# Gated linear attention and a channel MLP on one core: the first product in 15 products for 18, and scores that follow the update of the batch ahead

## The chip, the cores and the metric

The kernel runs on one core of a Trainium2 chip. The metric is the device time of one execution in microseconds (us). The engines are TensorE (PE in the profile, with its weight loads as PEld), VectorE (DVE), ScalarE (ACT), GpSimd (POOL) and SyncE (SP), which issues the DMAs.

## What is computed

The reference has two parts. The first is recurrent attention with a decay per element, for 4 batches, 8 heads, 768 positions and head size 48:

```
for t in range(S):
    state = alpha[:, :, t, :, None] * state + np.einsum('bhd,bhe->bhde', k[:, :, t], v[:, :, t])
    y[:, :, t] = np.einsum('bhd,bhde->bhe', q[:, :, t], state)
```

y becomes x of shape (4, 768, 384), and the second part is

```
xn = (x - mu) / np.sqrt(var + 1e-06) * g_ln
ch = np.maximum(xn @ w_ch1, 0.0) @ w_ch2
return x + ch
```

with mean and variance over the 384 features, w_ch1 of 384 x 1536 and w_ch2 of 1536 x 384. The weights arrive as 64-bit floats and are rounded to fp32 on the chip; everything else is fp32.

## The kernel before

**Tiles.** The 768 positions are cut into 6 chunks of 128. `attention(c, b)` (L205) is a generator that does one chunk of one batch in 16 pieces: logarithm of alpha (la); its running sum as a matmul with a triangle (lps) and two exponentials; k times one of them on GpSimd (L218); q times the other on VectorE (L220) and one row to DRAM; the loads of the next chunk's alpha, k, q, v (L227); two transposes (tps, L233, to qkT); the scores (aps, L245); their masked copy (L249); the row back as gate columns (L254); y (yps, L262 and L267); the state's update as a matmul (sps, L277); the update's sum on VectorE (L282) and its product with the gate on GpSimd (L284); statistics; the normalised x (xn, L295); its transpose into xT (L302).

**First product** (x times w1, then Relu, into hT). For chunks 0 and 1 `hidden` (L308) does 12 blocks of 3 matmuls of 512 columns. For chunks 2 to 5 `hidden_product` (L453) uses Winograd's form of Strassen's scheme on two of the three feature blocks: batches in halves, hidden blocks in halves, 7 products of a pair of blocks, of which 4 take the third feature block along in a second matmul. One group is 7 products, 22 matmuls of 256 columns; a chunk has 3 groups. `combine_first` (L404) makes the weights' sums on GpSimd; `combine_x` (L436) makes those of xT on VectorE at each chunk's start. Products leave PSUM by VectorE sums (L473, L481, L482, L484, L488) or ScalarE copies (L471, L475, L478), some are added further on GpSimd (L476, L479), and ScalarE does the Relu in place (L486, L490).

**Second product** (hT times w2). For chunk 0 `project` (L322) is direct; for chunks 1 to 5 `product` (L361) does Strassen's 7 products for each pair of batches, 6 matmuls of 192 columns each (L371). `combine_weights` (L337) makes w2's sums on GpSimd, `combine_hidden` (L349) those of hT on VectorE.

**Order.** The start (attention of chunks 0 and 1, rounding of the weights, `hidden(0)`) follows a string written by hand, ORDER, of one letter per piece (L23, L536). From then on `run(main, side)` (L523) goes through the main steps (second product of chunk c, first product of chunk c+1) and puts side steps (pieces of the attention of chunk c+2) between them in proportion. `attention_steps` (L495) gives 20 side steps: stages of 5, 2, 3, 5 and 1 pieces, with batch b one stage behind batch b-1. These calls set priorities; the tile framework then lays out each engine's order, in which an instruction that is ready can go ahead of one written earlier. An example: the logarithm of chunk 2's first batch runs at 34.59 us, while the first product of chunk 0 begins at 40.76.

**Buffers.** A tile's tag has a number of buffers; a new tile waits until an old one's last reader is done. a, k and q have 4 buffers each, v has 8 (L101). `combine_first` takes 2 of each of them for good, for its new sums. The 'm' tag of PSUM has 3 buffers, used by both products. hT has one.

Of the kernel before, what the change touches and what calls it, by code (L numbers as in the profile page):

```python
# [30 lines left out]
def kernel(  # L31
# [34 lines left out]

    nc = tc.nc
# [29 lines left out]
    def load(c, b, names="akqv"):  # L97
        for n, src in (("a", alpha), ("k", k), ("q", q), ("v", v)):
            if n not in names:
                continue  # L100
            t = raw.tile([P, H, D], FP32, name=f"r{n}", tag=f"r{n}",  # L101
                         bufs=2 * B if n == "v" else B)
            nc.sync.dma_start(t, src[b, c * P:(c + 1) * P])
            raws[n, c, b] = t
# [100 lines left out]
    def attention(c, b):  # L205
# [20 lines left out]
        if c + 1 < NCB:  # L226
            load(c + 1, b)  # L227
# [52 lines left out]
        if c + 1 < NCB:  # L280
            for i, s in heads:
                nc.vector.tensor_add(sts[b][s, :, i], sps[s], sts[b][s, :, i])  # L282
            st = sts[b].rearrange("p a b d -> p a (b d)")
# [53 lines left out]
    def combine_weights():  # L337
        b11, b12 = w2[:, :HJ, :HM], w2[:, :HJ, HM:]
        b21, b22 = w2[:, HJ:, :HM], w2[:, HJ:, HM:]
        t1, t2, t4 = (stage.tile([P, NF, 2 * P], INT64, name="ws", tag="ws")  # L340
                      .rearrange("p a c -> p (a c)").bitcast(FP32)[:, :HJ * HM]
                      .rearrange("p (a c) -> p a c", c=HM) for _ in range(3))
# [6 lines left out]
    def combine_hidden(c, b):  # L349
# [3 lines left out]
        sums = work.tile([P, 3, HJ, P], FP32, name="sums", tag="sums", bufs=1)  # L353
        s2, s3, s4 = (sums[:, i] for i in range(3))
# [6 lines left out]
    def product(c, b, n):  # L361

        if n == 1:
            combine_hidden(c, b)
            for i in (0, 1):
                win["o", i] = work.tile([P, 2, HM], FP32, name="ob", tag="ob", bufs=3)
            for i in range(4):
                win["u", i] = work.tile([P, HM], FP32, name=f"u{i}", tag=f"u{i}", bufs=1)
# [33 lines left out]
    HB = B // 2  # L402

    def combine_first():  # L404
        a11, a12 = w1[:, 0, :HJ * P], w1[:, 1, :HJ * P]
        a21, a22 = w1[:, 0, HJ * P:], w1[:, 1, HJ * P:]
        d1, d2 = w1[:, 2, :HJ * P], w1[:, 2, HJ * P:]
        parts = [[raw.tile([P, H, D], FP32, name=f"r{n}", tag=f"r{n}",
                           bufs=2 * B if n == "v" else B).rearrange("p h d -> p (h d)")
                  for _ in range(2)] for n in "akqv"]  # L410
        half = HJ // 2 * P

        def sub(outs, x, y):
            for i, o in enumerate(outs):
                cs = slice(i * half, (i + 1) * half)
                nc.gpsimd.tensor_sub(o, x[cs] if isinstance(x, list) else x[:, cs], y[:, cs])

        def blocks(x):
            if isinstance(x, list):
                return lambda j: x[j // (HJ // 2)][:, j % (HJ // 2) * P:][:, :P]  # L420
            return lambda j: x[:, j * P:(j + 1) * P]

        s2, s3, s4, dd = parts
        sub(dd, d1, d2)
        sub(s3, a11, a21)
        nc.gpsimd.tensor_add(a21, a21, a22)
        sub(s2, a21, a11)
        for i, o in enumerate(s4):
            nc.gpsimd.tensor_sub(o, a12[:, i * half:(i + 1) * half], s2[i])
        first_of["a"] = {n: blocks(x) for n, x in  # L430
                         ((1, a11), (2, a12), (3, s4), (4, a22), (5, a21), (6, s2), (7, s3))}
        first_of["d"] = {n: blocks(x) for n, x in ((2, d1), (3, dd), (4, d2), (5, d2))}

    first_of = {}

    def combine_x(c):  # L436
        xT = xT_of[c].rearrange("p f b t -> p f (b t)")
        lo, hi = slice(0, HB * P), slice(HB * P, B * P)
        b11, b12, b21, b22 = xT[:, 0, lo], xT[:, 0, hi], xT[:, 1, lo], xT[:, 1, hi]
        t = work.tile([P, 3, HJ * P], FP32, name="xs", tag="sums", bufs=1)  # L440
        t = t.rearrange("p a b -> p (a b)")
        t1, t2, t4 = (t[:, i * HB * P:(i + 1) * HB * P] for i in range(3))
        for i in range(3):
# [130 lines left out]
```

## Time and profile before

| | us |
|---|---|
| median of 3 runs | 496.3 |
| lowest and highest | 496.2, 497.53 |
| the profiled execution's own time | 495.51 |
| its span (first to last instruction) | 493.7 |

The mean granted TensorE clock of that execution was 0.999. A line of the profile gives the line of the code, the engine, the operation, tile written <- tiles read, shape and count; then busy time and mean duration of one, and behind a bar the engine's idle time just before such instructions, with what ended most of it. The chain of waits, followed back from the last instruction, is 79% TensorE, 13% VectorE, 4% DMA and 2% ScalarE; its largest parts are L371 (28%), L463 (15.4%), L466 (8.4%) and L313 (7.6%). TensorE's first instruction waits for alpha at 5.25 us.

### The profile page before, as it was taken

What the parts mean: (1) busy time and instruction counts of PE and PEld (TensorE: products, weight loads), DVE (VectorE), ACT (ScalarE), POOL (GpSimd) and SP (SyncE); (2) the same over time, 40 slices, a digit from 0 to 9 for tenths busy, and PEclk for the clock granted to TensorE, in tenths of its full rate; (3) what the DMA queues carried; (4) which work ended last, traced back from release to release, by engine and by line L of the source; (5) the groups of instructions that cost most, each with busy time, mean ns of one, the idle gap of its engine ahead of it and who ended that gap; (6) DMA issues with size and microseconds to landing.
All of it is one profiled execution on the core that took longest, in us unless ns stands there. A gap on an engine that the chain in (4) does not pass through costs nothing.

```text
span 493.7 us, 9035 instructions
## 1 busy us (share of the span) xinstructions
PE 477.2 (97%) x3712; PEld 385.9 (78%) x3712; DVE 284.0 (58%) x478; ACT 152.8 (31%) x325; POOL 131.7 (27%) x132
## 2 busy tenths in 40 slices
PE   4989999979999999999999999999999999999997
PEld 2766465546555599988889988889998889998997
DVE  4799998882433357565475555555654445443551
ACT  5573452530212221143441134342124431024300
POOL 5052000155210128532222222223123222222321
PEclk9999999999999999999999999999999999999999
DMA  8995726312200002211003212001200000000000
GB/s 281 342 243 174 256 91 201 109 50 65 65 2 1 29 5 64 81 56 28 17 18 118 52 56 65 1 1 32 66 33 2 1 0 1 34 32 1 1 33 32
DMA packets 32497, 33.83 MB, mean 69 GB/s; under 512 B 13108, under 2 KB 28596, under 8 KB 32456
## 3 DMA queue, kind: packets, MB, share of 16 engines
q1 hardware_dynamic: 31912, 33.12, 21.5%
q8 instruction: 29, 0.48, 0.4%
q10 hardware_dynamic: 544, 0.13, 0.1%
q14 instruction: 12, 0.10, 0.1%
HBM read 28.49 MB, written 4.76 MB: 67 GB/s over the span
## 4 chain that ended last, share of the span: by engine, by line
PE 79%; DVE 13%; DMA 4%; ACT 2%; issue 1%; SPq 0%; DVEq 0%; ACTq 0%
PE ops L371 28%; PE hps L463 15%; PE hps L466 8%; PE hps L313 8%; PE ops L326 4%; PE aps L245 4%; PE yps L267 3%; PE yps L262 3%; PE tps L233 3%; DVE ws L156 2%; DMA ws<-in_moe_w_ch_dram 2%; PE lps L212 2%; DVE w L163 2%; DVE w L150 1%; DVE at L249 1%; DVE w L159 1%
## 5 line engine op out<-in xcount | busy, mean ns | idle before, releaser
L313 PE MATMUL hps<-xT,w 128*128 128x512 f32 x144 | 66.1, 600 | 0.3 <-DVE w L163 0.2
L284 POOL TENSOR_TENSOR st<-st,gate 128x384 f32<-128x384 f32 x20 | 18.0, 899 | 127.2 <-DVE st L282 60.9
L313 PEld LDWEIGHTS hps<-xT,w 128*128 128x128 f32 x144 | 25.9, 190 | 27.8 <-issue 24.2
L371 PE MATMUL ops<-w,hT 128*128 128x192 f32 x240 | 44.1, 329 | 0.0
L466 PE MATMUL hps<-xT,w 128*128 128x256 f32 x144 | 42.8, 379 | 0.0
L371 PE MATMUL ops<-ws,hT 128*128 128x192 f32 x240 | 42.6, 326 | 0.0
L371 PE MATMUL ops<-w,sums 128*128 128x192 f32 x240 | 42.6, 327 | 0.0
L371 PEld LDWEIGHTS ops<-w,hT 128*128 128x128 f32 x240 | 39.2, 190 | 2.1 <-ACT hT L490 0.6
L371 PEld LDWEIGHTS ops<-w,sums 128*128 128x128 f32 x240 | 39.4, 190 | 1.8
L371 PEld LDWEIGHTS ops<-ws,hT 128*128 128x128 f32 x240 | 39.6, 190 | 0.0
L218 POOL TENSOR_TENSOR qk<-rk,ek 128x384 f32<-128x384 f32 x24 | 26.7, 1111 | 41.6 <-ACT ek L215 41.6
L249 DVE COPY_PREDICATED at<-consts,aps 128x512 f32<-128x512 int32 x48 | 32.3, 723 | 7.6 <-PE aps L245 7.4
L326 PE MATMUL ops<-w,hT 128*128 128x384 f32 x96 | 33.7, 494 | 2.7 <-DVE w L159 2.3
L476 POOL TENSOR_TENSOR xs<-xs 128x512 f32<-128x512 f32 x12 | 15.2, 1267 | 78.3 <-ACT xs L475 78.3
L267 PE MATMUL yps<-rv,at 128*64 128x48 f32 x768 | 35.8, 219 | 0.3 <-ACT x L270 0.3
L220 DVE TENSOR_TENSOR qk<-rq,eq 128x384 f32<-128x384 f32 x24 | 22.5, 942 | 23.0 <-ACT eq L216 23.0
L267 PEld LDWEIGHTS yps<-rv,at 128*64 128x64 f32 x768 | 31.6, 138 | 1.1 <-DMA ra<-in_alpha_dram 0.5
L282 DVE TENSOR_TENSOR st<-sps,st 64x192 f32<-64x192 f32 (+1 forms) x40 | 14.2, 354 | 29.6 <-PE sps L277 29.1
L466 PEld LDWEIGHTS hps<-xT,w 128*128 128x128 f32 x144 | 27.4, 190 | 3.7
L245 PEld LDWEIGHTS aps<-qkT 48*128 48x128 f32 x384 | 23.8, 187 | 8.3 <-issue 5.5
L326 PEld LDWEIGHTS ops<-w,hT 128*128 128x128 f32 x96 | 17.4, 190 | 14.7 <-DVE w L159 3.5
L262 PE MATMUL yps<-st,qkT 112*64 112x96 f32 x320 | 28.8, 258 | 0.0
(98 smaller groups left out, 849.3 us busy)
## 6 DMA issues: line engine op xcount, KB each, us to landing
ws<-in_moe_w_ch_dram SPq DMA_DIRECT2D x12, 768.0 KB, 8.4
ra<-in_alpha_dram SPq DMA_DIRECT2D x24, 192.0 KB, 3.1
rk<-in_k_dram SPq DMA_DIRECT2D x24, 192.0 KB, 2.4
rq<-in_q_dram SPq DMA_DIRECT2D x24, 192.0 KB, 2.5
rv<-in_v_dram SPq DMA_DIRECT2D x24, 192.0 KB, 2.9
out_dram<-ob SPq DMA_DIRECT2D x24, 192.0 KB, 2.3
row<-eq SPq DMA_DIRECT2D x20, 2.0 KB
gate<-row SPq DMA_DIRECT2D x20, 2.0 KB, 3.1
```

What stands on the lines that cost most here:

```text
L218: nc.gpsimd.tensor_mul(qk[:, 1, :, :D], raws.pop(("k", c, b)), ek)
L220: nc.vector.tensor_mul(qk[:, 0, :, :D], raws.pop(("q", c, b)), eq)
L245: nc.tensor.matmul(aps[i][:, p], qkT[rows, 1, p], qkT[rows, 0, p], start=True, stop=True)
L249: nc.vector.copy_predicated(out=at[:, i], data=aps[i], mask=mask.unsqueeze(1).broadcast_to([P, NP, P]))
L262: nc.tensor.matmul(yps[s, p].rearrange("p a b -> p (a b)"), qkT[:, 0, p, s], sts[b][:R, p].rearrange("p a b -> p (a b)"), start=True, stop ...
L267: nc.tensor.matmul(yps[s, p, i], at[:, i, p, s], vt[:, 2 * p + i], start=(c == 0), stop=(c == 0 or i == 1))
L284: nc.gpsimd.tensor_mul(st, st, gate.unsqueeze(2).broadcast_to([P, NP, 2 * D]))
L313: nc.tensor.matmul(hps, w1[:, f, j * P:(j + 1) * P], xT_of[c][:, f], start=(f == 0), stop=(f == NF - 1))
L326: nc.tensor.matmul(ops_of[b], hT_of[c][:, j, b], w2[:, j], start=(j == 0), stop=(j == NJ - 1))
L371: nc.tensor.matmul(acc, win["a"][n][:, j], win["b"][n][:, j], start=(j == 0), stop=(j == HJ - 1))
L463: nc.tensor.matmul(acc[:, i], first_of["a"][n](j + i), first_of["b"][n], start=True, stop=n not in first_of["d"])
L466: nc.tensor.matmul(acc[:, i], first_of["d"][n](j + i), first_of["x"][n], start=False, stop=True)
```

## The change

It has these parts:

1. **First product in 15 products for 18.** Features are cut in thirds (the three feature blocks), hidden blocks in thirds (4 each), batches in halves. A direct product of such blocks is 3 x 3 x 2 = 18 block products; the new scheme has 15. `hidden_product(c, r, n)` does one product of two hidden blocks as 2 matmuls of 256 columns; a chunk has 2 groups (r) of 15. It is used from chunk 1 on (before: from chunk 2). A group before had 7 + 4 matmuls per block, which is 11 of 12.
2. **Sums.** `combine_first` has 17 sums or differences of w1's blocks on GpSimd, each as two instructions of 384 and 128 columns; 6 new blocks lie in two buffers each of a, k and q (and a small tile for the remaining columns), the rest in place of w1. It is called ahead of chunk 0's run, not after it. `combine_x` has 11 VectorE instructions of 256 columns for 4.
3. **Evictions.** Of 15 products 12 leave by a VectorE instruction and 3 by a ScalarE copy; 7 further sums are on GpSimd; 6 Relus of two instructions of 256 columns follow. The order of the products is FIRST.
4. **Tiles.** `combine_hidden`'s three sums get a tile each for one together, two of which `combine_x` takes again; the small u tiles are laid into three of 512 columns; the weights' staging tiles are taken once, as `spare`.
5. **combine_weights** becomes a step between chunk 0's second product and chunk 1's first.
6. **v** is loaded behind the update's VectorE sum, not with a, k and q, and has 4 buffers for 8. This is in `attention`, so it holds for the start too.
7. **attention_steps.** 23 side steps for 20, some empty. A batch's y and update, then the scores (with masked copy and gate) of the next batch, then the rest up to xn of the first are one step.

The core of the diff:

```diff
-                         bufs=2 * B if n == "v" else B)
+                         bufs=B)
...
-            load(c + 1, b)
+            load(c + 1, b, "akq")
...
                 nc.vector.tensor_add(sts[b][s, :, i], sps[s], sts[b][s, :, i])
+            load(c + 1, b, "v")
...
     def combine_first():
...
+        extra = cpool.tile([P, 6, P], FP32, name="extra")
+        a = [w1[:, f, t * NT * P:(t + 1) * NT * P] for t in range(3) for f in range(NF)]
+        a = [(x[:, :3 * P], x[:, 3 * P:]) for x in a]
+        new = [(raw.tile([P, H, D], FP32, name=f"r{n}", tag=f"r{n}", bufs=B)
+                .rearrange("p h d -> p (h d)"), extra[:, 2 * i + k])
+               for i, n in enumerate("akq") for k in range(2)]
...
+        n3, n9, n5, n0, n1, n11 = new
+        do(sub, n3, a[3], a[7])
+        do(add, n5, n3, a[5])
+        do(add, n9, n3, a[8])
+        do(sub, n0, a[1], a[3])
+        do(sub, n1, n0, a[5])
+        do(sub, n0, n0, a[4])
+        do(sub, a[4], a[3], a[4])
+        do(add, a[4], a[4], a[5])
+        do(sub, a[5], a[0], a[7])
+        do(sub, n11, a[2], a[8])
+        do(sub, n11, n11, n5)
+        do(add, a[8], a[5], a[8])
+        do(sub, a[5], a[5], a[6])
+        do(sub, a[6], a[8], a[5])
+        do(sub, a[6], a[6], a[7])
+        do(add, a[2], a[2], a[0])
+        do(sub, a[2], a[2], a[1])
...
     def combine_x(c):
...
+        t100, t101, t103 = (t[:, HJ * HM:][:, :HB * P] for t in spare)
+        t102, m7, m8, m9, m10, m13 = new
+        sub(t101, b[1], b[3])
+        sub(t100, b[4], b[5])
+        add(t103, b[2], t100)
+        add(m7, t101, t103)
+        sub(t102, b[0], t100)
+        sub(m10, t102, t101)
+        sub(t101, t101, b[5])
+        sub(m9, b[0], b[4])
+        add(b[4], b[2], b[4])
+        sub(m13, t103, b[3])
+        sub(m8, t102, b[1])
...
+    FIRST = (3, 7, 5, 10, 9, 1, 4, 14, 11, 6, 13, 2, 8, 0, 12)
+
+    def hidden_product(c, r, n):
...
+        a, b = first_of["a"][n], first_of["b"][n]
         for i in range(2):
+            j = 2 * r + i
+            w = a[0][:, j * P:(j + 1) * P] if j < 3 else a[1]
+            nc.tensor.matmul(acc[:, i], w, b, start=True, stop=True)
...
+        if n == 3:
+            nc.scalar.copy(out=c5, in_=acc)
+        elif n == 7:
+            add(c4, acc, c5)
+        elif n == 5:
+            add(c2, acc, c4)
+        elif n == 1:
+            add(u0, acc, c2)
+        elif n == 10:
+            nc.scalar.copy(out=u1, in_=acc)
+        elif n == 9:
+            sub(u2, u1, acc)
+            add_late(c4, c4, u2)
+        elif n == 4:
+            sub(c2, c2, acc)
+            add_late(c2, c2, u1)
+            relu(c2)
+        elif n == 14:
+            add(u2, acc, u2)
+            add_late(c0, u0, u2)
+        elif n == 6:
+            add(c4, acc, c4)
+            relu(c4)
+        elif n == 11:
+            nc.scalar.copy(out=c1, in_=acc)
+            add_late(c0, c0, c1)
         elif n == 2:
+            add(c0, acc, c0)
+            relu(c0)
+        elif n == 13:
+            sub(c3, u0, acc)
+            add_late(c1, c1, c3)
+        elif n == 8:
+            sub(u2, u2, acc)
+            add_late(c1, c1, u2)
+            relu(c1)
+            add_late(c5, c5, u2)
+        elif n == 0:
+            sub(c3, c3, acc)
+            relu(c3)
         else:
+            sub(c5, c5, acc)
+            relu(c5)
...
-        stages = [5, 2, 3, 5, 1]
...
+        for b in range(-3, B + 1):
+            moves = [(b, 2), (b + 1, 3), (b, 3)]
+            steps.append([m for m in moves if 0 <= m[0] < B])
+            steps += [[]] if b > 1 else []
+            steps += [[(i, n)] for i, n in ((b - 1, 1), (b + 2, 2), (b + 3, 5)) if 0 <= i < B]
...
-        if c > 1:
+        if c > 0:
...
+    spare = [stage.tile([P, NF, 2 * P], INT64, name="ws", tag="ws")
+             .rearrange("p a c -> p (a c)").bitcast(FP32) for _ in range(3)]
+    combine_first()
     for c in range(NCB):
         side = attention_steps(c + 2) if c + 2 < NCB else []
-        run(project_steps(c) + hidden_steps(c + 1), side)
-        if c == 0:
-            combine_weights()
-            combine_first()
+        steps = project_steps(c) + ([combine_weights] if c == 0 else [])
+        run(steps + hidden_steps(c + 1), side)
```

## The prediction, made before the result was known

> **What bounds the kernel now.** I read the page first, then busy time by stage, then the groups of instructions with shapes kept apart, then TensorE's timeline. The page:
>
> ```profile
> PE 477.2 (97%) x3712; PEld 385.9 (78%) x3712; DVE 284.0 (58%) x478; ACT 152.8 (31%) x325; POOL 131.7 (27%) x132
> PE   4989999979999999999999999999999999999997
> DVE  4799998882433357565475555555654445443551
> ```
>
> TensorE is full from the 10th slice (111 us) on. Stages cut at the products' borders (columns: stretch, its length, busy us of each engine):
>
> ```profile
> 84.00:108.50 24.50, 20.47 (x91) 11.83 (x88) 22.09 (x31) 9.82 (x22) 7.17 (x5) 1.00 0.31 89
> 131.00:174.00 43.00, 42.98 (x316) 23.27 (x315) 15.04 (x29) 9.73 (x22) 4.43 (x5) 1.00 0.08 24
> 287.00:330.00 43.00, 43.00 (x402) 36.94 (x401) 23.39 (x43) 16.84 (x37) 11.29 (x10) 1.00 0.09 25
> 434.50:463.00 28.50, 28.50 (x134) 25.09 (x133) 11.42 (x19) 10.62 (x19) 7.60 (x6) 1.00 0.03 10
> ```
>
> Only 84 to 108.5 (VectorE still rounds w2, 22.1 of 24.5 us busy) is not TensorE's. 131 to 174 is the first product of chunk 1, 287 to 330 that of chunk 3 with attention beside it, 434.5 to 463 that of chunk 5 alone. In these TensorE never idles, so a matmul taken out there is worth its issue interval, as long as nothing else becomes late. The groups concerned (busy, mean ns of one | idle before it):
>
> ```profile
> L313 PE MATMUL hps<-xT,w 128*128 128x512 f32 x144 | 66.1, 600 | 0.3 <-DVE w L163 0.2
> L466 PE MATMUL hps<-xT,w 128*128 128x256 f32 x144 | 42.8, 379 | 0.0
> L476 POOL TENSOR_TENSOR xs<-xs 128x512 f32<-128x512 f32 x12 | 15.2, 1267 | 78.3 <-ACT xs L475 78.3
> L473 DVE TENSOR_TENSOR hT<-hps,xs 128x512 f32<-128x512 f32 x12 | 8.3, 692 | 7.1 <-PE hps L466 6.2
> L490 ACT ACTIVATE hT<-hT 128x512 f32<-128x512 f32 x24 | 13.8, 624 | 9.0 <-DVE hT L488 9.0
> ```
>
> A matmul is two instructions here. Their means (600, 379 ns) overlap; the interval between starts is what counts.
>
> **What the Trainium skill says.** "TensorE: Matmul & The Clock Gate", Back-to-back issue gap, gives an isolated gap of some N/2.4 ns. In the trace 12 instructions of 512 columns (6 matmuls) take 5.15 us, 0.43 each, and one of 256 columns takes 0.216: in proportion to the columns as the page says, but at twice its figure, and a matmul is two of them. "TensorEngine Tiling (Array Packing)", Key Properties, says that changing the tiling mode drains TensorE; the trace agrees, about 0.1 us each way (below). "SBUF — State Buffer", SBUF: two separate sides, says that a GpSimd instruction and a VectorE one with two SBUF inputs exclude each other for a whole instruction. The trace agrees: L156, 0.95 us elsewhere, takes 3.38 beside a GpSimd instruction of 2.79.
>
> ```profile
> 101.61 2.79 POOL L343 TENSOR_TENSOR ws<-w 128x1152 f32<-128x1152 f32 x1 [0.90 <-DVE w L159]
> 101.85 3.38 DVE L156 SCALAR_TENSOR_TENSOR ws<-ws 128x768 int32<-128x768 int32 x1
> ```
>
> VectorE's evictions from PSUM have one SBUF input, and stay at 0.69 us beside GpSimd.
>
> **The change, part by part**, against the profiled execution's 495.5 us (span 493.7; the median of the three runs is 496.3).
>
> *Matmuls removed.* Chunk 5 issues 3 groups x 22 = 66 matmuls of 256 columns in 28.49 us (434.36 to 462.85), 0.4317 us each. After it is 2 groups x 15 products x 2 = 60, or 25.90 us: 2.59 saved, in chunks 2 to 5 10.36. Chunk 1: 36 matmuls of 512 columns at 0.859 us = 30.9 against 25.9, 5.0 saved. Together **-15.4**, all on the path.
>
> *Scores behind y and update.* Now they stand apart, with products between them:
>
> ```profile
> 206.35 0.63 PE L277 MATMUL sps<-rv,qk 128*64 128x48 f32 x16
> 206.91 2.22 PE L371 MATMUL ops<-w,sums 128*128 128x192 f32 x12
> 209.06 1.16 PE L245 MATMUL aps<-qkT 48*128 48x128 f32 x16
> 210.15 1.56 PE L463 MATMUL hps<-xT,w 128*128 128x256 f32 x6
> ...
> 72.52 1.16 PE L245 MATMUL aps<-qkT 48*128 48x128 f32 x16
> ```
>
> From 206.91 to 209.06 twelve instructions take 2.15 us; undisturbed ones take 1.95. So leaving the update and entering the scores cost 0.2 together. At 72.52 scores follow an update directly (71.96 + 0.56 us), and no gap shows. Three batches of four in each of chunks 2 to 5 gain 0.2: **-2.4**. Bounds: 0 if the engine's order pulls them apart again, -2.4 as said.
>
> With these alone the time is 495.5 - 17.8 = 477.7.
>
> *More work off TensorE.* A chunk has 24 VectorE evictions for 15, +9 x 0.69 = 6.2 us; combine_x 11 instructions for 4, +7 x 0.42 = 2.9; GpSimd 14 late additions for 6, +8 x 1.27 = 10.2; ScalarE 6 copies for 9, and 24 Relus of 256 columns for 12 of 512. No Relu of 256 columns is in the trace: 0.31 us (half of 0.62) to 0.62; "VectorE: DVE Perf Modes" (its section on the errata) prices ScalarE at 224 + columns cycles of 1.2 GHz, an estimate of 0.40, which I take: about +0.4 us. In a first product with attention VectorE goes from 23.4 busy us of 43 to some 33 of 40, GpSimd from 11 to 21, ScalarE stays below 20. None is full, so nothing here costs by sum. combine_x has TensorE's last two second-product steps to hide under (3.9 us from when the sums that it overwrites come free, for some 4 instructions of 0.42 until product 3 can start); without that cover it would cost about 2 us a chunk.
>
> *Order within a group.* A product takes TensorE 0.86 us, its eviction 0.69, with three PSUM buffers. I walked the group in order: only the end is tight. The last product's eviction (n=12) needs GpSimd's third sum in a row, behind c1+=c3 and c1+=u2: it can run some 1.75 us after its matmuls end. One of three buffers is held that long, and the next group's first evictions are behind it on VectorE, its next matmuls behind those. From zero (attention or the other buffers hide it) to 1.75 us, in 10 groups: 0 to 17.5. In the sided chunks TensorE has attention to do meanwhile, and the next group's first product leaves by ScalarE; I take 0.15 a group, **+1.5**.
>
> *combine_first before chunk 0's run.* It had all of chunk 1; now its 34 GpSimd instructions must be ready for hidden(1). A pair (384 and 128 columns) is 1.0 to 1.3 + 0.35 to 0.45: L416 takes 1.0 alone. 17 pairs: about 26 us. GpSimd has room for it (7.2 busy of 24.5 us, then 11.3 of 22.5, of which combine_weights is 11.4). But six results go to buffers of a, k and q that come free only as chunk 2's batches are consumed (in this trace a at 90.5 and 100.4; k at 90.2, 100.7, 113.0 and 133; q at 92.0, 105.7, 109.5 and 133.4). n0 and then n1 are a chain through these: n1 will likely have its buffer only from the last batch, about 133, and nine pairs follow it (n1, n0, a4 twice, a5, a8, a5, a6 twice), some 15 us until product 6 can run, about 148. TensorE, which reaches hidden(1) at about 126 as attention's steps are spread thinner, has until then five products, y, scores and transposes (some 15 of 22 us), and makes up part of the rest since attention is then done. **+3**, from 0 (buffers come earlier) to 12 (little is there to fill).
>
> *combine_first beside the rounding.* Between 90 and 108 GpSimd gets three or four pairs more; each VectorE instruction of two SBUF inputs can wait for one of them, 0.4 to 1.3 us. The end of the rounding releases TensorE (0.94 us idle at 108.5 for L159). **+1**, from 0 to 3. combine_weights, now a step ahead of hidden(1), is needed only at 174: nothing.
>
> *v's load later*, behind the update instead of with a, k, q, with 4 buffers for 8. On SP's queue it waits for TensorE's update of the same batch, already issued then; behind it stand weights' loads and rows of gates. Chunk 1's v, now loaded from 12.8 to 26.5 us, would come at about 20 to 33; its first y is at 35.8, a landing takes 2.9 us. The early DMA is full (85% busy up to 40 us), so up to 1 us may be gained there. **0**, from -1 to +1.
>
> Sum: 495.5 - 15.4 - 2.4 + 1.5 + 3 + 1 = 483.2; I say **483**.
>
> **Rivals.**
> *All of it hidden:* 477.7, or 478. For: TensorE never waited on the same sort of chain before (two GpSimd sums ahead of L481) while doing 0.86 us products. Against: the walk through the group, and the a, k, q buffers.
> *GpSimd's chain shows at each group's end:* 1 us of the 1.75 in 10 groups, 10 - 1.5 more: 491.7. For: chunk 5's groups have no attention to fill, and VectorE keeps order. Against: in four of the five chunks attention fills.
> *Slower: the late buffers of combine_first.* If loads of chunk 3 take the freed buffers of k and q before n0 and n1 ask (the trace shows such loads going out early, at 43 us), n1 waits for the first batch of chunk 3 to be consumed, and hidden(1) stands still at its sixth product. The price: about 17 us of attention work fills 131 to 148, then TensorE idles until some 168 to 171: 20 to 23 us, 477.7 + 23 = 501. It decides as soon as TensorE idles over 17.8 us between 126 and 170. Against: chunk 3's attention can itself be brought forward when TensorE is free.
> That the matmuls don't disappear can't be: their number is in the program.
>
> **How the numbers follow.** Likeliest (480 to 488) 0.52, all hidden 0.22, chain at group ends 0.15, late buffers 0.11. About 0.3% (1.5 us) is what a measurement can tell from no change. Faster: 0.52 + 0.22 + 0.12 of the third = 0.86; same 0.03; slower 0.11. The range takes in all hidden with v's gain (477) and the chain up to 493; it leaves out the last case and the tail of the third, some 0.15.
>
> **What would show it.** In the profile after: 600 matmul instructions of 256 columns in the first products of chunks 1 to 5 and 72 of L313's form left (right for the first step); chunk 5's first product near 26 us without idle TensorE (group end hidden) or near 28 (not); scores straight behind updates with 0.56 us between their starts; TensorE's idle time between 126 and 170 below 5 us, with what ended it being GpSimd on the weights' sums (buffers). I am wrong if VectorE is above 90% busy in a first product with matmuls waiting for it, or if the part before 84 us moves by more than 1 us.

## The result, and the profile after

The changed kernel takes **491.78 us** (median of 4 runs, 491.57 to 492.5) against 496.91 (496.2 to 498.14) for the kernel before on the same chip: a ratio of 0.9897, 95% interval 0.9871 to 0.9922. It is faster by 5.1 us, where the forecast's sum had 12.3. The profiled execution took 492.5 us, its span is 490.7.

The page of the changed kernel, the lines that answer to those shown of before:

```profile
PE 466.2 (95%) x3712; PEld 389.5 (79%) x3712; DVE 342.5 (70%) x571; ACT 158.4 (32%) x385; POOL 215.9 (44%) x203
PE   4989999785999999999999999999999999999997
DVE  3799999879067678568778567868576766565751
PEclk9999999998899999999999999999999999999999
```

TensorE was full from the 10th slice on; now the 8th to the 10th have a hole (7, 8, 5), and the granted clock dips in the 10th and the 11th. GpSimd went from 131.7 busy us to 215.9. The stages (stretch, its length, busy us of TensorE, weight loads, VectorE, ScalarE, GpSimd, then the granted clock):

```profile
88.05:108.50 20.45, 16.83 (x61) 9.79 (x60) 17.30 (x27) 8.35 (x18) 7.62 (x8) 1.00 0.26 77
108.50:136.36 27.86, 21.94 (x72) 12.41 (x70) 15.78 (x18) 0.00 (x0) 27.55 (x19) 0.88 0.07 22
288.24:331.87 43.63, 43.59 (x459) 37.31 (x458) 30.97 (x54) 18.40 (x48) 21.82 (x19) 1.00 0.18 53
432.07:459.76 27.69, 26.90 (x121) 22.47 (x121) 16.11 (x24) 9.54 (x24) 15.97 (x14) 1.00 0.04 15
```

The second line is the odd one: from 108.5 to 136.4 us GpSimd is busy throughout (27.55 of 27.86), TensorE idles 5.9 us, and its clock averages 0.88. The groups that the change made, shapes kept apart (busy, mean ns of one | idle before it):

```profile
L315 PE MATMUL hps<-xT,w 128*128 128x512 f32 x72 | 33.0, 601 | 0.3 <-DVE w L164 0.2
L485 PE MATMUL hps<-xT,w 128*128 128x256 f32 x120 | 31.5, 385 | 0.0
L493 ACT ACTIVATE hT<-hT 128x256 f32<-128x256 f32 x120 | 42.9, 409 | 55.6 <-POOL hT L510 23.6 <-POOL hT L529 13.0 <-DVE hT L522 10.7
```

The 512-column matmuls fell from 144 instructions to 72; the L485 rows of all operands add up to 600. Cut at the borders of the products, a stage being timed from its first matmul to the next stage's first, the profiled runs compare like this (e1, e9 and e10 are experiments below):

| us | before | after | e1 | e9 | e10 |
|---|---|---|---|---|---|
| start to chunk 0's first product | 40.76 | 43.12 | 42.63 | 42.80 | 41.86 |
| chunk 0, first product | 43.30 | 44.93 | 44.16 | 43.31 | 44.16 |
| chunk 0, second product | 47.14 | 48.31 | 40.05 | 38.62 | 40.06 |
| chunk 1, first product | 43.09 | 44.98 | 46.41 | 44.94 | 46.43 |
| chunk 1's second to chunk 5's first product | 288.56 | 278.42 | 278.45 | 278.41 | 277.23 |
| chunk 5, second product, to the end | 30.85 | 30.94 | 31.00 | 30.72 | 30.86 |
| span | 493.7 | 490.7 | 482.7 | 478.8 | 480.6 |

From chunk 1's second product on, the change gives 10.14 us. Nearly all that is missing is missing before that: the first four rows became 7.05 us longer, where matmuls worth 5.0 had gone from the fourth. TensorE's timeline of the changed kernel shows the largest piece:

```profile
106.53 0.91 PE L328 MATMUL ops<-w,hT 128*128 128x384 f32 x2 [1.54 <-DVE w L160]
...
111.34 5.43 PE L328 MATMUL ops<-w,hT 128*128 128x384 f32 x16
122.69 12.66 PE L328 MATMUL ops<-w,hT 128*128 128x384 f32 x32 [5.92 <-DVE ob L332]
```

TensorE stands 5.92 us, in the middle of chunk 0's second product, until the eviction L332 frees a PSUM buffer. Why L332 is late stands in VectorE's timeline of the same stretch:

```profile
111.06 0.42 DVE L453 TENSOR_TENSOR ws<-xT 128x256 f32<-128x256 f32 x1
111.51 2.72 DVE L454 TENSOR_TENSOR ws<-xT,ws 128x256 f32<-128x256 f32 x1
114.15 1.22 DVE L456 TENSOR_TENSOR sum<-xT,ws 128x256 f32<-128x256 f32 x1
...
120.96 1.21 DVE L462 TENSOR_TENSOR sum<-sum,xT 128x256 f32<-128x256 f32 x1
122.09 1.01 DVE L332 TENSOR_TENSOR ob<-ops,x 128x384 f32<-128x384 f32 x2
```

and in GpSimd's:

```profile
106.61 7.34 POOL L343 TENSOR_TENSOR ws<-w 128x1152 f32<-128x1152 f32 x1 [5.34 <-DVE w L160]
113.91 1.18 POOL L219 TENSOR_TENSOR qk<-rk,ek 128x384 f32<-128x384 f32 x1
...
117.32 1.17 POOL L418 TENSOR_TENSOR rq<-w 128x384 f32<-128x384 f32 x1
118.45 1.17 POOL L418 TENSOR_TENSOR rk<-rk,w 128x384 f32<-128x384 f32 x1
```

Ten of the eleven combine_x instructions of chunk 1 were let in ahead of two evictions of chunk 0, as soon as their inputs were there (the eleventh, L459, had run at 75 us). Alone each takes 0.42 us. Here seven take 1.21 or 1.22, about the interval at which GpSimd's sums start: the two engines take turns, one instruction each. One (L454) takes 2.72, until L343 of combine_weights ends. So the evictions come at 122.09. They could have come at about 114 and 117: e1 below, where TensorE is 1.3 us further ahead at this point, has ScalarE doing them at 112.96 and 115.54.

### The profile page after: what moved, and what is told of

It reads as the page before. It is cut to its first block, busy times and chain, and to the rows that moved or that the text cites. A ratio compares the mean times of both kernels' runs of the same rounds, so it can differ in the third digit from the quotient of the medians.

```text
span 490.7 us, 9312 instructions
## 1 busy us (share of the span) xinstructions
PE 466.2 (95%) x3712; PEld 389.5 (79%) x3712; DVE 342.5 (70%) x571; ACT 158.4 (32%) x385; POOL 215.9 (44%) x203
## 4 chain that ended last, share of the span: by engine, by line
PE 75%; DVE 17%; issue 3%; ACT 3%; POOL 1%; DMA 1%; SPq 0%; DVEq 0%; POOLq 0%; ACTq 0%
PE ops L372 28%; PE hps L485 24%; PE tps L234 4%; PE aps L246 4%; PE hps L315 3%; PE yps L268 3%; PE ops L328 3%; PE lps L213 3%; PE yps L263 2%; DVE at L250 2%; DVE w L151 1%; DVE ws L157 1%; DVE qk L221 1%; PE sps L278 1%; DVE w L164 1%
## 5 line engine op out<-in xcount | busy, mean ns | idle before, releaser
L493 ACT ACTIVATE hT<-hT 128x256 f32<-128x256 f32 x120 | 42.9, 409 | 55.6 <-POOL hT L510 23.6
L485 PE MATMUL hps<-sum,w 128*128 128x256 f32 x200 | 51.9, 382 | 0.2
L372 PE MATMUL ops<-w,sum 128*128 128x192 f32 x240 | 42.3, 326 | 0.0
L485 PEld LDWEIGHTS hps<-sum,w 128*128 128x128 f32 x200 | 37.1, 190 | 6.2 <-DVE hT L516 0.9
L372 PEld LDWEIGHTS ops<-w,sum 128*128 128x128 f32 x240 | 39.6, 190 | 0.8
L315 PE MATMUL hps<-xT,w 128*128 128x512 f32 x72 | 33.0, 601 | 0.3 <-DVE w L164 0.2
L507 POOL TENSOR_TENSOR hT<-hT,u 128x512 f32<-128x512 f32 x10 | 12.8, 1276 | 44.4 <-DVE u L506 44.4
L485 PE MATMUL hps<-xT,w 128*128 128x256 f32 x120 | 31.5, 385 | 0.0
L246 PE MATMUL aps<-qkT 48*128 48x128 f32 x384 | 28.8, 285 | 0.7 <-DVE at L250 0.5
L237 ACT COPY qkT<-tps 112x512 f32<-112x512 f32 x32 | 18.3, 586 | 33.3 <-PE tps L234 33.0
```

The costliest lines, as they stand in the source:

```text
L237: nc.scalar.copy(out=qkT[:, i], in_=tps)
L246: nc.tensor.matmul(aps[i][:, p], qkT[rows, 1, p], qkT[rows, 0, p], start=True, stop=True)
L315: nc.tensor.matmul(hps, w1[:, f, j * P:(j + 1) * P], xT_of[c][:, f], start=(f == 0), stop=(f == NF - 1))
L372: nc.tensor.matmul(acc, win["a"][n][:, j], win["b"][n][:, j], start=(j == 0), stop=(j == HJ - 1))
L485: nc.tensor.matmul(acc[:, i], w, b, start=True, stop=True)
L493: nc.scalar.activation(out=x[:, i], in_=x[:, i], func=AFT.Relu)
```

## Experiments

The theory on which most of them were made: the loss is a queue on VectorE (combine_x ahead of the evictions), and the GpSimd sums, which the change calls earlier, make that queue three times as long. Rivals: a cost in the last chunk's group ends, the order of the side steps, late buffers of combine_first, or a gain that the edit would bring to any kernel. All medians are of several runs beside the kernel before on the same chip; the ratio is always to the kernel before.

**e1: the evictions leave VectorE's queue.**

```diff
-            nc.vector.tensor_add(ob, ops_of.pop(b), x_of.pop((c, b)))
+            nc.scalar.copy(out=ob, in_=ops_of.pop(b))
+            nc.vector.tensor_add(ob, ob, x_of.pop((c, b)))
```

> Chunk 0's second product leaves PSUM by a ScalarE copy, and VectorE adds x to it afterwards in SBUF; nothing else is changed. Theory (queue): VectorE's two first evictions of chunk 0's second product stand behind the 11 combine_x instructions of chunk 1, each of which waits for a GpSimd sum; TensorE then waits for PSUM from 116.8 to 122.7 us and runs slow for some us after it. With the copy on ScalarE, idle since 108 us, that wait goes: 483 to 485 us, and combine_x still takes about 1.2 us an instruction. Rival (rounding): what was lost is that GpSimd's sums slow the rounding of the weights before 110 us: then 490 to 492 us, TensorE's wait only moves. Rival (steady): the loss is in the first products of chunks 2 to 5: no change, 491 to 492 us.

Measured: **484.65 us**, ratio 0.9746 (0.9724 to 0.9769). The timelines of TensorE, ScalarE and VectorE in e1 (its lines below L332 are one further down):

```profile
110.07 15.75 PE L328 MATMUL ops<-w,hT 128*128 128x384 f32 x48
112.90 1.22 DVE L457 TENSOR_TENSOR sum<-xT,ws 128x256 f32<-128x256 f32 x1
112.96 0.48 ACT L332 COPY ob<-ops 128x384 f32<-128x384 f32 x1 [5.94 <-PE ops L328]
...
115.54 0.48 ACT L332 COPY ob<-ops 128x384 f32<-128x384 f32 x1 [2.10 <-PE ops L328]
```

combine_x is as slow as before (1.22), but no eviction of chunk 0 waits for it: 48 instructions run through in 15.75 us where the changed kernel had 16, a hole, and 32. Chunk 0's second product and chunk 1's first together take 86.46 us for 93.29, 6.8 less; that is most of the 8.0 between the spans (the other 1.3 lie in the start and in chunk 0's first product, where the two programs are the same). The edit has a price of its own: VectorE's addition behind the copy (L333 in e1) now has both inputs in SBUF, takes 2.24 us at 126.37 beside a GpSimd sum, and holds TensorE up by 1.0 us through the masked copy that stands behind it. This is most of why chunk 1's first product is 1.4 us longer in e1 than in the changed kernel.

**e5: the same edit on the kernel before.** The diff is e1's.

> The kernel before (496.9 us), with the same edit as in e1: the direct product's output tile is copied out by ScalarE and VectorE adds x afterwards. Queue theory (the edit repairs what the change put ahead of these evictions, the eleven sums of combine_x): the kernel before has four such sums, 0.42 us each, so nothing much is repaired, 495.5 to 497.5. Rival (the edit is a gain of its own, VectorE being busy with the rounding in that stretch): 488 to 492. The profile also shows the start: with the same program up to 40 us as before, the first direct product begins at 40.8 us if the start of the changed kernel is really slower, near 42.5 if the start varies from run to run.

Measured: 497.65 us, ratio 1.0008 (0.9993 to 1.0022): no gain. The two stages take 90.23 us, exactly as before. So the edit is worth nothing in itself; it repairs what the change did. The start: the first product begins at 41.93 us, with a program that up to there is the one that began at 40.76.

**e6: no GpSimd sums in combine_first.**

```diff
-                op(out[i], x[i], y[i])
+                nc.scalar.copy(out=out[i], in_=x[i])
```

> The changed kernel with the 34 sums of combine_first replaced by ScalarE copies of their first operand (the sums are left out, so the first products of chunks 1 to 5 are other numbers); TensorE's and VectorE's orders stay as they are. Contention theory (combine_x's instructions take 1.21 us only because each shares the SBUF port with a GpSimd sum): the eleven take 0.42 to 0.6 us each while no GpSimd sum runs, the two evictions behind them come some 6 us earlier, TensorE's wait of 5.9 us before 122.7 shrinks to 1 or less, 483 to 486. Rival (it is the number of instructions ahead and when their inputs are ready, not the port): the wait stays at 4 us or more, 489 to 492.

Measured: 488.78 us, ratio 0.982 (0.9794 to 0.9846), 0.2 below the rival's range, with the wait unchanged (5.99 us). But the condition of the experiment wasn't met, as e6's VectorE and GpSimd show:

```profile
112.07 2.84 DVE L455 TENSOR_TENSOR sum<-ws 128x256 f32<-128x256 f32 x1
114.83 2.83 DVE L457 TENSOR_TENSOR sum<-sum,ws 128x256 f32<-128x256 f32 x1
117.58 0.41 DVE L460 TENSOR_TENSOR xT<-xT 128x256 f32<-128x256 f32 x1
...
118.93 1.01 DVE L332 TENSOR_TENSOR ob<-ops,x 128x384 f32<-128x384 f32 x2
```

```profile
111.83 2.80 POOL L344 TENSOR_TENSOR ws<-w,ws 128x1152 f32<-128x1152 f32 x1
114.71 2.67 POOL L345 TENSOR_TENSOR ws<-w,ws 128x1152 f32<-128x1152 f32 x1
```

combine_weights moved up into the room that combine_first left. Three instructions of VectorE took 2.7 to 2.8 us, one for each GpSimd sum of 1152 columns, and when those were over the next took 0.41. The experiment doesn't tell the theories apart; e9 takes these sums out too. What it does show: chunk 0's first product is back at 43.30 us, so what it has over that with the sums comes from them: 1.6 us in the changed kernel, 0.9 in e1 and e3, which are the same program up to there.

**e9: no GpSimd sums at all there.** e6's edit, and in combine_weights:

```diff
-        nc.gpsimd.tensor_sub(t1, b12, b11)
-        nc.gpsimd.tensor_sub(t2, b22, t1)
-        nc.gpsimd.tensor_sub(t4, b21, t2)
-        nc.gpsimd.tensor_sub(b12, b22, b12)
+        nc.scalar.copy(out=t1, in_=b12)
+        nc.scalar.copy(out=t2, in_=b22)
+        nc.scalar.copy(out=t4, in_=b21)
+        nc.scalar.copy(out=b12, in_=b22)
```

> The changed kernel with the sums of combine_first and of combine_weights both replaced by ScalarE copies of one operand (the sums are left out, so the products of chunks 1 to 5 are other numbers); GpSimd has almost nothing left between 88 and 125 us. VectorE keeps the eleven sums of combine_x ahead of chunk 0's evictions. If the SBUF port shared with GpSimd is what makes the eleven slow: they take 0.42 us each, some 5 us together for 12.3, the evictions come 7 us earlier, TensorE's 5.9 us wait falls below 1, and the time is 481 to 485. If it is the queue alone (the eleven wait for their inputs or for the rounding): the eleven still end some 12 us after their first, the wait stays at 4 us or more, 487 to 490.

Measured: 480.6 us, ratio 0.9669 (0.9645 to 0.9693), 0.4 below the expected range. VectorE in e9:

```profile
108.61 0.43 DVE L454 TENSOR_TENSOR ws<-xT,ws 128x256 f32<-128x256 f32 x1
108.95 0.42 DVE L456 TENSOR_TENSOR sum<-xT,ws 128x256 f32<-128x256 f32 x1
...
110.63 0.42 DVE L461 TENSOR_TENSOR sum<-ws,xT 128x256 f32<-128x256 f32 x1
110.97 0.55 DVE L332 TENSOR_TENSOR ob<-ops,x 128x384 f32<-128x384 f32 x1
```

The ten take 4.0 us from first start to last end, and the first eviction stands behind nine of them at 110.97, with TensorE not waiting.

**e12: both edits**, e1's and e9's.

> e1's edit and e9's together (the sums of combine_first and combine_weights left out): what is left when neither the queue nor the shared port costs. Theory: e1's first direct product of chunk 0 gets 0.9 us shorter (43.3 us as in the kernel before), and chunk 0's second product and chunk 1's first together fall from 86.5 to 84.5 to 85.5; in all 481 to 483, and within 1.5 us of e9. Rival (the port costs beyond what the queue passes on): 3 us or more below e1, 478 to 481.

Measured: 479.69 us, ratio 0.9658 (0.9632 to 0.9685), within 1.0 us of e9. It completes a table of two by two. Chunk 0's second and chunk 1's first product together take

| us | evictions behind combine_x | evictions on ScalarE |
|---|---|---|
| GpSimd sums beside it | 93.29 (after) | 86.46 (e1) |
| no GpSimd sums | 83.56 (e9) | 83.58 (e12) |

Most of the loss takes both: the queue costs 6.8 us with the sums and nothing without; the sums cost 9.7 with the queue and 2.9 without. What was forecast for these two rows without any loss is 90.23 - 5.0 - 0.6 = 84.6. Of e12's expectation the first product of chunk 0 is right (43.30), but the time lies in the rival's range: without the sums 3.8 us more go than the queue had passed on, 2.9 in these two stages and 0.9 in the first product.

**e8: combine_first called later**, on e1's kernel (behind four of the twelve steps of chunk 0's second product).

```diff
-    combine_first()
     for c in range(NCB):
...
+        if c == 0:
+            steps.insert(4, combine_first)
```

> e1's kernel (484.65) with combine_first called behind the fourth step of chunk 0's second product, and not ahead of the first. Theory that the sums beside the rounding cost what the prediction gave them (some 1 to 2 us between 60 and 105 us) and that their buffers are in time: 482.5 to 484. Rival: what is gained there is lost by sums that come late for chunk 1's first product, which has TensorE waiting for GpSimd: 485.5 to 489. Third: GpSimd takes the same sums at the same times since it goes by when inputs and buffers are there, no difference.

Measured: 491.42 us, ratio 0.9881 (0.9857 to 0.9906); the rival, and worse than it said. Chunk 0's first product is no shorter (44.26), and chunk 1's takes 53.45 us for 46.41. TensorE in e8:

```profile
139.12 1.13 PE L486 MATMUL hps<-xT,w 128*128 128x256 f32 x4 [2.12 <-POOL w L419]
142.09 2.08 PE L486 MATMUL hps<-sum,w 128*128 128x256 f32 x4 [1.84 <-POOL w L419]
154.84 1.70 PE L486 MATMUL hps<-sum,w 128*128 128x256 f32 x4 [2.21 <-DVE hT L517]
```

Two of these waits, 4.0 us together, are for combine_first's sums. This is what the prediction feared, now brought about; in the changed kernel itself TensorE idles 0.4 us in that stage, in e1 1.4, and there it waits for no sum of GpSimd.

**e10: the group end of chunk 5**, on e1's kernel. In chunk 5 the sum for c5 goes ahead of that for c1 on GpSimd, and VectorE copies the next group's first product out:

```diff
+            if c == NCB - 1:
+                add_late(c5, c5, u2)
             add_late(c1, c1, u2)
             relu(c1)
-            add_late(c5, c5, u2)
+            if c < NCB - 1:
+                add_late(c5, c5, u2)
...
-            nc.scalar.copy(out=c5, in_=acc)
+            (nc.vector.tensor_copy if c == NCB - 1 else nc.scalar.copy)(out=c5, in_=acc)
```

> e1's kernel (484.65) with an end of a group made shorter in chunk 5 only: GpSimd's sum for c5 ahead of that for c1, and the first product of a group evicted by VectorE, not by ScalarE behind the Relus. Theory that the group end in chunk 5 holds TensorE 0.7 to 0.85 us, and ScalarE's queue is what replaced it in e3: chunk 5's first product 26.8 to 27.0 us for 27.7, in all 483.5 to 484.3. Rival (VectorE or the third PSUM buffer is late next): 27.5 or more, no difference.

Measured: **482.68 us**, ratio 0.9721 (0.969 to 0.9751), the fastest kernel here that computes everything. Chunk 5's first product takes 26.5 us (and 26.5 again in e13, which has the same edit), better than expected; that is 1.2 us, and the rest of the 2.0 between the medians of e10 and e1 is not explained by the edit (the profiled start was 0.8 us earlier). The intervals of e1 and e10 overlap, so it is the profile, not the medians, that shows this gain.

**e3: only the order of the two sums**, on the changed kernel, in all chunks.

```diff
         elif n == 8:
             sub(u2, u2, acc)
+            add_late(c5, c5, u2)
             add_late(c1, c1, u2)
             relu(c1)
-            add_late(c5, c5, u2)
```

> Behind product 8 GpSimd adds u2 into c5 first and into c1 second, so the last product's eviction waits for one sum less. Theory: the chain at a group's end costs TensorE some 1.3 us in chunk 5's middle (about 0.9 and 0.3 of idle time there) and little where attention fills: 0.5 to 2 us faster, 490 to 491.3 us, and the idle time at 447 us in chunk 5 gone. Rival: the Relu of c1, now one sum later, holds something else up: no change or slower.

Measured: 492.28 us, ratio 0.9887 (0.9873 to 0.9902): no effect. The wait moved. First the changed kernel, then e3, at the border of chunk 5's two groups:

```profile
447.09 0.69 DVE L536 TENSOR_TENSOR hT<-hT,hps 128x512 f32<-128x512 f32 x1 [1.74 <-POOL hT L531]
...
447.83 0.70 PE L485 MATMUL hps<-xT,rk 128*128 128x256 f32 x2 [0.69 <-DVE hT L536]
```

```profile
445.26 0.69 DVE L536 TENSOR_TENSOR hT<-hT,hps 128x512 f32<-128x512 f32 x1 [0.46 <-POOL hT L529]
...
446.49 1.64 ACT L493 ACTIVATE hT<-hT 128x256 f32<-128x256 f32 x5 [1.24 <-POOL hT L530]
...
448.04 0.56 ACT L496 COPY hT<-hps 128x512 f32<-128x512 f32 x1
...
448.65 1.13 PE L485 MATMUL hps<-sum,w 128*128 128x256 f32 x4 [1.19 <-ACT hT L496]
```

Counted from the stage's first matmul, the last eviction came 1.3 us earlier (13.74 us for 15.02), but now five Relus, the first of which waits for GpSimd's other sum, stand in ScalarE's queue ahead of the next group's first copy. e10 takes both away.

**e4: the side steps of before**, all else as after.

```diff
-        steps = []
-        for b in range(-3, B + 1):
...
+        stages = [5, 2, 3, 5, 1]
+        return [lambda t=turns[b], n=stages[w - b]: [next(t) for _ in range(n)]
+                for w in range(B + len(stages) - 1)
+                for b in range(B) if 0 <= w - b < len(stages)]
```

> Attention's side steps as in the kernel before (20 steps, stages of 5, 2, 3, 5, 1), all else as changed. Theory: scores no longer follow an update directly, which costs 0.2 us for each of 12 batches, 2.4 us; but attention of chunk 2 comes earlier, and so do the a, k and q buffers that the weights' sums wait for, which can win up to 1 us: 492.5 to 494 us. Rival: the wider spread of the side steps is what made chunk 1's first product start late (136 us for 131): then faster by 2 to 5 us.

Measured: 506.54 us, ratio 1.0192 (1.0165 to 1.0219): 14.8 us slower than the changed kernel, far outside. The old steps bring chunk 2's attention earlier, into the stretch that is already short of VectorE: chunk 0's second product takes 57.87 us, in which TensorE waits 7.6 us for the rounding and 6.6 for L332. But also from chunk 1's second product to chunk 5's, where nothing of that plays, it takes 285.43 us for 278.42.

**e7: the new side steps, cut apart**, on e1's kernel.

```diff
-            steps.append([m for m in moves if 0 <= m[0] < B])
+            steps += [[m] for m in moves if 0 <= m[0] < B]
```

> e1's kernel (484.65) with the merged side step (y and update, scores, rest) cut into its parts, so that products come between them again, in the new order. Theory that directness is what counts (one mode switch into and out of the scores, 0.2 us, twelve times, a little more through lost cover): chunks 1 to 5 from the second product of chunk 1 take 280.5 to 282 for 278.45, in all 487 to 489. Rival (the order and the spacing of the moves count, not that they are merged): with more steps attention is spread otherwise, 283 to 286 for that part as in e4, 490 to 493. Third: no difference, 484 to 485.5.

Measured: 496.24 us, ratio 0.9983 (0.9971 to 0.9995). For the part from chunk 1's second product to chunk 5's the directness theory is right: 280.87 us for 278.45, 2.4 for nine batches, 0.27 each. Here the windows (busy us in the order TensorE, weight loads, VectorE, ScalarE, GpSimd) of e7 and of e4:

```profile
181.13:462.00 280.87, 279.66 (x2207) 251.49 (x2206) 192.71 (x328) 86.81 (x223) 118.37 (x109) 1.00 0.13 38
```

```profile
187.88:473.31 285.43, 280.71 (x2208) 251.50 (x2207) 188.02 (x331) 83.74 (x224) 122.48 (x109) 1.00 0.12 37
```

e7 has TensorE 2.1 us longer busy than e1 (277.53), with 1.2 idle for 0.9; this fits the mode switches, at which TensorE counts as busy. e4 has 3.2 more busy and 4.7 idle, 0.9 of which e1 has too: more than half of what the old order loses is waiting. The total of e7 misses both theories, because the more numerous steps brought attention forward into chunk 0's second product: 54.65 us for 40.05, with TensorE waiting 5.53 us for the rounding, while chunk 1's first product got 6.2 shorter.

**e2: chunk 1 keeps its direct form**, 15 products from chunk 2 on, with combine_weights and combine_first behind chunk 0's run.

> Chunk 1's first product goes back to the 36 direct matmuls of 512 columns, and the sums of both weights are made after chunk 0's run, as in the kernel before; chunks 2 to 5 stay in 15 products. Theory (queue): this gives back 5.0 us of matmuls, but takes away the sums beside the rounding (1.6 us), the wait for PSUM and the slow TensorE after it (7.6 us) and late buffers (1 us): 486 to 488 us, faster than the changed kernel though it does more. Rival (steady): the loss is in chunks 2 to 5; then the matmuls count alone and it is 496 to 497 us.

Measured: 497.73 us, ratio 1.0009 (0.9986 to 1.0032), 10 us over what was expected. No clean test: chunk 0's first product is back at 43.30 us, but chunk 2's first product takes 50.84 us for 43.64, with 5.1 idle. GpSimd, VectorE and TensorE in e2:

```profile
208.82 6.62 POOL L418 TENSOR_TENSOR w<-w 128x384 f32<-128x384 f32 x6
215.40 0.59 POOL L389 TENSOR_TENSOR ob<-u,x 128x192 f32<-128x192 f32 x1
216.02 0.36 DVE L393 TENSOR_TENSOR ob<-ops,ob 128x192 f32<-128x192 f32 x1 [2.23 <-POOL ob L389]
216.43 1.13 PE L485 MATMUL hps<-sum,w 128*128 128x256 f32 x4 [2.74 <-DVE ob L393]
```

combine_first's sums (L418), which now run beside the end of chunk 1's second product, stand ahead of that product's own late additions on GpSimd (L389); VectorE's eviction waits for those, and TensorE for the eviction. A second wait of the same kind, 2.30 us, ends at 220.51. It is the queue of the changed kernel once more, on another engine. Besides, chunk 0's second product takes 51.34 us, having more side steps beside it since a direct chunk 1 has fewer steps to spread them over.

**e13: combine_weights later**, on e10's kernel, to clear the stretch of e9 without leaving anything out.

```diff
-        steps = project_steps(c) + ([combine_weights] if c == 0 else [])
-        run(steps + hidden_steps(c + 1), side)
+        steps = project_steps(c) + hidden_steps(c + 1)
+        if c == 0:
+            steps.insert(len(project_steps(c)) + 10, combine_weights)
+        run(steps, side)
```

> e10's kernel (482.7) with combine_weights called behind the tenth step of chunk 1's first product and not at the end of chunk 0's second: its first instruction, which took 7.3 us and held VectorE's third combine_x instruction for 2.7, no longer lies beside the end of the rounding. Port theory: chunk 0's second product 38.7 to 39.5 us for 40.06, chunk 1's first product unchanged at 46.4 or less, in all 481 to 482.3 (start alike). Rival: GpSimd has no room later, its sums for w1 or w2 come late and TensorE waits in chunk 1's first product, 48 us or more there, 484 to 487. Third: combine_first's sums move up into the place and hold VectorE the same, no difference.

Measured: 491.03 us, ratio 0.9865 (0.9838 to 0.9892): 8 us worse than e10, worse than any theory said. VectorE in e13:

```profile
107.47 1.75 DVE L157 SCALAR_TENSOR_TENSOR ws<-ws 128x768 int32<-128x768 int32 x1
...
114.09 1.74 DVE L160 SCALAR_TENSOR_TENSOR w<-w,ws 128x768 f32<-128x768 f32 x1
```

The third theory's mechanism, with a price nobody gave it: combine_first's sums of 384 columns moved up beside the end of the rounding, whose instructions went from 0.95 to 1.75 us, and TensorE waited 4.09 us for L160 at 115.89, where e1 and e10 run through. Chunk 0's second product takes 46.09 us for e10's 40.06, chunk 1's first 47.66 for 46.43; another 2.0 us lie in the start and chunk 0's first product, before the edit. In the changed kernel the long combine_weights instruction (106.61, 7.34 us) stood ahead of them on GpSimd, and VectorE ran at its own speed beside it for five of these microseconds.

## Why the prediction was wrong, point by point

The sign, and the range, held; the size didn't. That the range held is luck in part: it went up to 493 for the sake of a rival, group ends, that didn't come true. Set against the prediction's own sum (483.2), the profiled execution (492.5) is 9.3 us over; the kernel before was profiled in one of its quickest executions, so the two profiled executions differ by 3.0 us where the medians differ by 5.1. By stage, forecast and measured (three of the twelve batches of scores and two of the ten groups lie in the third row, the others in the fourth; the +1 for sums beside the rounding is in the third, since the prediction placed them between 90 and 108 us):

| us | forecast | measured | over |
|---|---|---|---|
| start | 0 | +2.36 | 2.4 |
| chunk 0, first product | 0 | +1.63 | 1.6 |
| chunk 0's second and chunk 1's first product | -5.0 - 0.6 + 0.3 + 3 + 1 = -1.3 | +3.06 | 4.4 |
| to chunk 5's second product | -10.36 - 1.8 + 1.2 = -11.0 | -10.14 | 0.8 |
| rest | 0 | +0.09 | 0.1 |

*Matmuls removed: right.* 600 and 72 instructions, in undisturbed stretches 0.216 us from one of the 600 to the next. *Scores behind update: right in size*, 0.27 a batch in e7 for the 0.2 forecast; in the profile scores follow an update at 0.56 us, as said (TensorE, changed kernel):

```profile
228.12 0.63 PE L278 MATMUL sps<-rv,qk 128*64 128x48 f32 x16
228.68 1.16 PE L246 MATMUL aps<-qkT 48*128 48x128 f32 x16
```

What the prediction didn't see is that the old order of the side steps would have cost the thinner kernel another 4 us of waiting (e4): undone alone, the two halves of the change are not a sum.

*More work off TensorE: right.* In chunk 3's first product VectorE is 31 us busy, GpSimd 22, ScalarE 18, forecast at 33, 21 and under 20; the 256-column Relu takes 0.409 us for the estimate of 0.40 that was worked out from the Trainium skill.

*Order within a group: right sum, wrong place.* Forecast 0.15 in each of ten groups, 1.5. Measured: chunk 5's first product takes 27.69 us against 25.9, 1.8 over, of which 1.3 lie at the border of its two groups, while the matching stages of chunks 2 to 4, with attention beside them, idle under 0.1. e10 recovers 1.2 of it.

*Late buffers: +3 was not paid.* TensorE idled 0.4 us there in the changed kernel, and not for a sum. Late sums do cost TensorE something (e8), but here the buffers and the sums came in time.

***The step that failed*** is the term "combine_first beside the rounding, +1, from 0 to 3", together with the sentences on the work off TensorE that "nothing here costs by sum" and that combine_x "has TensorE's last two second-product steps to hide under". Measured in their place: with combine_x ahead of the evictions, GpSimd's early sums cost 9.7 us in chunk 0's second and chunk 1's first product (93.29 against 83.56 in e9), and 0.9 to 1.6 in chunk 0's first. Each of the two missed a part of the same thing. The first looked only for rounding instructions that wait for a sum, between 90 and 108 us; the sums run from 58 to 135. The second took combine_x at 0.42 us an instruction and asked who waits for combine_x, namely product 3. Nobody asked who stands *behind* it on VectorE. Those are two evictions of the stage that still runs, and combine_x's instructions have two SBUF inputs like the rounding's. Ten of them, most at 1.21, take from 109.85 to 122.09 in front of the evictions, with one rounding instruction in between. e9 shows the sums as the cause of its length, e1 the queue as the way to TensorE, and the two-by-two table that it takes both.

The Trainium skill's page "SBUF — State Buffer", section SBUF: two separate sides, which the prediction had named, says that such instructions of VectorE and GpSimd exclude each other for a whole instruction; the trace agrees (1.21 for 0.42), and it was applied to one stretch only. The section names VectorE's faster modes that use two ports too, not just two inputs, and the trace agrees here as well: L149, with one SBUF input, takes 0.55 us elsewhere and 1.36 at 74.06, beside a sum of combine_first that runs for 1.18 from 73.82. The prediction left those out.

*The start.* That the part before 84 us moves by more than 1 us was said to be a mark of error, and it moved by 4.0: 1.6 in chunk 0's first product and 2.4 in the start. Much of the 2.4 isn't the change's: the old program began its first product at 40.76 and at 41.93 us (e5), changed ones at 41.02 (e12) to 43.40 (e6), depending on whether twelve early transposes take 1.5 us or 2.3 to 2.8; both occur with the old program and with changed ones, and why is open. But a part is: in all twelve profiles of changed programs an update at about 30 us (L278) waits 0.8 to 1.7 us for VectorE's sum of the state (L283), and in neither of the two profiles of the old program does it. Short transposes compared with short, changed programs begin 0.3 to 1.1 us later, long with long 0.6 to 1.5. Which part of the change brings this was not tried. That *v's later load* costs nothing was not tried by itself either; no instruction in the profile after waits for it.

Of the rivals, *group ends* came to the right total (491.7) by the wrong way: it put 10 us there, where 1.3 are.

## What to carry to other kernels

When work is moved to a free engine or called earlier, ask for each new instruction not only who waits for it but who stands behind it in its engine's order, and price it as it runs beside the others' work, not alone: here 0.42 us became 1.21, and the queue behind it turned that into TensorE's time. Keep evictions that free TensorE's buffers, and additions that these evictions wait for (e2), out of the queue of an engine that also does work with no hurry. And a scheduler may fill the hole that you make: taking sums out of a stretch (e6) or moving them later (e13) pulled other sums in, so look at what comes in their place before you count the gain.

## What the runs showed of the hardware that was not expected

*An idle TensorE pays twice.* The windows of the changed kernel around its wait (the eighth figure, behind GpSimd's, is the granted clock):

```profile
116.00:122.00 6.00, 0.77 (x3) 0.15 (x1) 6.00 (x6) 0.00 (x0) 5.92 (x7) 0.84 0.00 0
122.00:126.00 4.00, 3.31 (x5) 1.85 (x6) 1.10 (x3) 0.00 (x0) 4.00 (x5) 0.50 0.27 97
126.00:130.00 4.00, 4.00 (x12) 2.35 (x11) 0.00 (x0) 0.00 (x0) 4.00 (x3) 0.89 0.01 5
```

After 5.9 us of idleness the clock is at half, and stays there for some 4 us of work: the 32 instructions behind the wait take 12.66 us, where 48 undisturbed ones in e1 take 15.75, or 10.5 for 32. So the wait cost about 2 us on top of its own 5.9. The Trainium skill's page "TensorE: Matmul & The Clock Gate", Part 1, says half rate after an idle window of about 3.4 us and full rate after a busy one as long; the trace agrees, with 0.50 for some 4 us after 5.9 idle.

*Who goes first where VectorE and GpSimd exclude each other.* Beside a single GpSimd instruction of 1152 columns (L343, 7.34 us in the records for 2.6 to 2.8 elsewhere) VectorE ran for five microseconds at its own speed; beside a row of GpSimd sums of 384 columns it got one instruction in between each two. These are readings of single stretches, and GpSimd's spans are rough.
